# Three w2 tiles' differences moved from GpSimd to VectorE, and the sums of an output block as five operations instead of seven

## The chip, the cores and the metric

The program runs on one core of a Trainium2 chip. The time is the device time of one execution in microseconds (us). Engines are named as the profile names them: PE is TensorE, DVE is VectorE, ACT is ScalarE, POOL is GpSimd, SP is SyncE, which only issues DMAs here.

## The reference

Three layers follow each other: a windowed attention, a dense layer with a rational activation, and a layer of eight experts, in which the change lies:

```
def _moe2_ref(x, w_gate, w1, w2):          # 2304 tokens, 512 wide, 8 experts, 1024 hidden
    ...                                    # P: softmax of x @ w_gate, balanced 8 times
    for e in range(E):
        h = np.maximum(x @ w1[e], 0.0)
        ye = h @ w2[e]
        out += P[:, e:e + 1] * ye
    return out
```

## The kernel before

All products of the expert layer run on PE in half precision, each number split in a high and a low half (three matmuls stand for one), and each block product is done by a scheme of seven products on sums and differences of blocks, where the plain way takes eight.

**Blocks.** An expert is taken for three groups of 768 tokens; v counts the 24 pairs of expert and group. The 1024 hidden columns of an expert are cut into four slices, so that m = 4v + i counts 96 steps. A *unit* is one of seven products of layer 1 of a step: six matmuls of 384 columns (`moe_l1`, line L924). 28 units later (`LG`) layer 2 follows, three products to a unit: for each v three blocks of 128 token rows (p), for each the four slices i, for each seven products x of three matmuls of 256 columns (`moe_l2`, L1015 to L1017). L1015 takes the high halves of both operands, L1016 the low half of w2. So 84 units of both layers make one expert, and when layer 2 goes from one expert to the next (its *turn*), the four new w2 tiles must be there.

**Weights.** A tile of w1 or w2 is loaded into one of two buffers `raw0`, `raw1` (`raw_load`; L844 to L846 for w2). `raw_diff` (L873) makes its four differences in one buffer `wd`; `raw_split` makes the high halves on ACT (L884) and the low halves on DVE (L887), the three raw blocks first (768 columns), then the four differences (1024 columns). k counts an expert's tiles: 0 to 3 of w1, 4 to 7 of w2. The differences of expert 0 are DVE's, those of experts 1 to 7 POOL's: 224 operations. `pin` puts each of these behind the last h of its group that stands before it in the program: on DVE behind L991, on POOL behind POOL's L946, on ACT behind L990. Five buffers hold split w2 tiles, so tiles 5 to 7 of an expert can be filled only as the last block of the expert before is used up, and `use` and `prep_at` place their work there, three units apart. `raw_absmax` (L850) reads each tile once more, half an expert ahead.

**Layer 1's results** go from PE's banks through ACT (L973, L980) and DVE (L975, L978, L983), ReLU on ACT (L976, L984), sums by `combine` (L946: three on DVE, one on POOL), then high halves on ACT (L990) and low halves on DVE (L991). A bank takes its next product only when the earlier one has been read.

**Layer 2's results.** When the seven sums p1 to p7 of a block stand in four banks, `y_evac` adds them up: one copy on ACT (L1034), then on DVE seven additions of 256 columns (L1036), each of a bank's half and a block in SBUF. `y_out` scales the result on ACT (L1045) and adds it to the output by a DMA of POOL's queue (L1050). There are 72 such blocks. The four banks are handed to the next block as they come free.

The order of the instructions on each engine is made by a scheduler that plays the program through with costs of its own; each engine then works in that order.

Of the kernel before, what the change touches and what calls it, by code (L numbers as in the profile page):

```python
# [16 lines left out]
ALU = mybir.AluOpType  # L17
# [11 lines left out]
def kernel(  # L29
# [14 lines left out]
    nc = tc.nc  # L44
# [5 lines left out]
    P = 128  # L50
# [53 lines left out]
    def room(tag, shape, dt):  # L104
        where, era, a, size = HOME[tag]
        n = math.prod(shape[1:]) * (2 if dt == F16 else 4)
        assert n <= size, (tag, shape)
        old = rooms.get(where)
        if old is None or old[0] < era:
            old = rooms[where] = era, sb.tile([P, ROOMS[where] // 4], F32R if era == 1 else F32, tag=where, name=f"room{where}")  # L110
        assert old[0] == era, (tag, old[0])
        t = old[1][0:shape[0], a // 4:(a + n) // 4]
        if dt != (F32R if era == 1 else F32):
            t = t.bitcast(dt)
        d = "abcd"[:len(shape) - 1]
        if len(d) > 1:
            t = t.rearrange(f"p ({' '.join(d)}) -> p {' '.join(d)}", **dict(zip(d[1:], shape[2:])))
        return t
# [698 lines left out]
    NP = NF2 // 2  # L817
    FH = FE // 2
    EH = DM // 2
# [8 lines left out]
    def pin(eng, i):  # L828
        if eng in behind:
            tc.add_manual_dep(i.ins, behind[eng], mybir.DependencyInfo(mybir.DependencyClass.Sync, mybir.DependencyReason.DATA), reason="after this group's h")  # L830
# [36 lines left out]
    def raw_diff(e, k, n):  # L867
        w = k // NP
        o, x, y = DIFFS[w][n]
        d = room("wd", [P, 4, EH], F32)  # L870
        a, b = ({"b": raw[e, k], "d": d}[z[0]][:, int(z[1]), :] for z in (x, y))
        eng = nc.gpsimd if e else nc.vector
        pin("p" if e else "v", eng.tensor_tensor(out=d[:, o, :], in0=a, in1=b, op=ALU.add if w == 0 and n == 0 else ALU.subtract))  # L873

    def raw_split(e, k):
        w, i = divmod(k, NP)
# [116 lines left out]
    yb = {}  # L993
# [1 line left out]
    later_u = []  # L995
    unit_now = [0]
    gate_ready = [False]
    PRODS = ((0, 0, 1, 0), (0, 1, 5, 4), (1, 0, 4, 3), (1, 1, 6, 5), (2, 0, 3, 1), (2, 1, 7, 2), (3, 0, 2, 6))
    NQ = NM * 3 * 7

    def moe_l2(q):
        s, x = divmod(q, 7)
        v, r = divmod(s, 3 * NP)
        p, i = divmod(r, NP)
        e, G = GV[v]
        h = mac[v * NP + i]["h"]
        hh, hl = h[:, 0], h[:, 1]
        if i == 0 and x == 0:
            for b in range(4):
                yb[b] = bank("yps", True)  # L1010
        w = w2s[e, i]
        b, half, a, m = PRODS[x]
        o = yb[b][:, half * EH:(half + 1) * EH]
        c = slice(p * P, (p + 1) * P)
        nc.tensor.matmul(o, hh[:, a - 1, c], w[:, m, 0, :], start=i == 0 and half == 0, stop=False)  # L1015
        nc.tensor.matmul(o, hh[:, a - 1, c], w[:, m, 1, :], start=False, stop=False)  # L1016
        nc.tensor.matmul(o, hl[:, a - 1, c], w[:, m, 0, :], start=False, stop=i == NP - 1 and (half == 1 or b == 3))  # L1017
        if i == NP - 1 and x == 6:
            y_evac(v, p)
# [7 lines left out]

    def y_evac(v, p):
        yd = room(f"yd{(3 * v + p) % 2}", [P, 2, DM], F32)
        d = yd[:, 1, :], yd[:, 0, :]  # L1030
        vv = room("yv", [P, EH], F32)
        p1, p6, p5, p7, p2, p3, p4 = (yb[b][:, h * EH:(h + 1) * EH] for b, h, _, _ in PRODS)
        u, x, w, z = d[0][:, 0:EH], d[0][:, EH:], d[1][:, 0:EH], d[1][:, EH:]
        nc.scalar.activation(u, p1, AF.Copy)  # L1034
        for o, s0, s1 in ((vv, p6, u), (x, p5, vv), (w, p7, vv), (z, p7, x), (u, p2, u), (x, p3, x), (w, p4, w)):
            nc.vector.tensor_tensor(out=o, in0=s0, in1=s1, op=ALU.add)  # L1036
        if gate_ready[0]:
            y_out(v, p, yd)
        else:
            pend.append((v, p, yd))  # L1040

    def y_out(v, p, yd):
        e, G = GV[v]
        for n in range(2):
            nc.scalar.activation(yd[:, n, :], yd[:, n, :], AF.Copy, scale=gate_col(e, 2 * TPB * G + TPB * n + p))  # L1045
        dst = bass.AP(out.tensor, (2 * TPB * G + p) * P * DM, [[DM, P], [TPB * P * DM, 2], [1, DM]])
        if e == 0:
            nc.sync.dma_start(out=dst, in_=yd)
        else:
            later_u.append((unit_now[0] + 2, lambda: pin("p", nc.gpsimd.dma_start(out=dst, in_=yd, accum_op=ALU.add))))  # L1050
# [66 lines left out]
    for b, s0, s1 in ATT:  # L1117
        pcs = att_pieces(b)
        n = 4 * (s1 - s0 + 1) - 4
# [50 lines left out]
    def prep_at(s, e, k, step):  # L1170
        for n in range(4):
            at(int(s + n * step), raw_diff, e, k, n)
        for n in range(4):
            at(int(s + (1, 2, 4, 5)[n] * step), raw_part, e, k)
        use.append((int(s + 5 * step), e, k, s))
# [71 lines left out]
    n = len(pcs)  # L1247
# [92 lines left out]
```

## Time and profile before

| | |
|---|---|
| time, median of 3 runs | 2047.74 us (2046.5 to 2050.35) |
| the profiled execution's own time | 2048.93 us |
| its span, first to last instruction | 2047.1 us |
| busy: PE, DVE, ACT, POOL | 1904.1, 1635.2, 1230.9, 551.0 us |
| mean granted clock of PE | 0.967 of full speed |

The expert layer's products begin some 750 us into the span and last to its end. In the profile's slices by time PE is busy 90% or more from 800 us on and its granted clock is full. The end of a matmul is modelled there, past the start of the next, so that a busy PE can still start late; the starts in the timeline are what counts.

### The profile page before, as it was taken

To read this page: it belongs to the slowest core of one execution; us is meant where nothing else is said; L and a number is where in the kernel's file an instruction comes from. 1 tells how busy PE (TensorE), PEld (TensorE's weight loads), DVE (VectorE), ACT (ScalarE), POOL (GpSimd) and SP (SyncE) were. 2 spreads that over 40 slices of the span, in tenths; PEclk is the share of its full clock that TensorE was granted. 3 is DMA by queue.
4 is the path that set the end of the run, shared out by engine and by line. 5 is a ranking of instruction groups with operands and counts; after the bars stand their busy time and mean duration, and the time that the engine had idled before them with its cause. 6 is when DMAs were issued, how large, how long until landed. Compare 5 with 4: busy or idle time off the path is not lost. (4 is left out here: it accounts for less than half of the span.)

```text
span 2047.1 us, 36511 instructions
## 1 busy us (share of the span) xinstructions
PE 1904.1 (93%) x13914; PEld 1433.2 (70%) x13914; DVE 1635.2 (80%) x2844; ACT 1230.9 (60%) x2328; POOL 551.0 (27%) x574
## 2 busy tenths in 40 slices
PE   7588899998989789999999999999999999999997
PEld 6466667776766557777777777777777777777776
DVE  5898899899998878787777877877877787787754
ACT  5677777776776545555555654655565565465542
POOL 1232233222222003122332431422333143142211
PEclk7788999999999899999999999999999999999999
DMA  6542220124310333245346344435534634533323
GB/s 173 163 139 77 60 75 13 33 66 140 104 42 11 119 126 96 68 128 149 63 108 172 77 116 130 93 83 123 139 63 116 166 75 116 139 84 84 77 57 48
DMA packets 209792, 200.07 MB, mean 98 GB/s; under 512 B 78288, under 2 KB 160208, under 8 KB 209616
## 3 DMA queue, kind: packets, MB, share of 16 engines
q1 hardware_dynamic: 192480, 164.70, 26.4%
q0 software_dynamic: 17136, 33.03, 10.8%
q8 instruction: 109, 1.79, 0.4%
q14 instruction: 67, 0.55, 0.1%
HBM read 151.67 MB, written 46.01 MB: 97 GB/s over the span
## 5 line engine op out<-in xcount | busy, mean ns | idle before, releaser
L924 PEld LDWEIGHTS <-roomA 128*128 128x128 f16 x3276 | 322.1, 99 | 199.4 <-issue 36.5
L924 PE MATMUL l1a<-roomA 128*128 128x384 f16 x1872 | 357.3, 328 | 11.2 <-ACT roomA L973 5.3
L924 PE MATMUL l1b<-roomA 128*128 128x384 f16 x1404 | 277.0, 330 | 12.1 <-DVE roomA L975 6.7
L873 POOL TENSOR_TENSOR roomA<-roomA 128x256 f32<-128x256 f32 x224 | 198.3, 912 | 104.5 <-DVE roomA L887 62.2
L683 POOL TENSOR_TENSOR roomIG<-roomA,roomIG 128x384 fp32r<-128x384 f32 x96 | 112.9, 1176 | 295.2 <-ACT roomIG L682 238.7
L1015 PE MATMUL yps<-roomA 128*128 128x256 f16 x630 | 170.5, 272 | 5.8 <-ACT roomA L884 3.8
L1016 PE MATMUL yps<-roomA 128*128 128x256 f16 x630 | 171.1, 273 | 3.4 <-DVE roomA L887 3.3
L1015 PE MATMUL yps<-roomA,roomV 128*128 128x256 f16 x630 | 171.2, 273 | 1.4 <-DVE roomA L1036 0.8
L1016 PE MATMUL yps<-roomA,roomV 128*128 128x256 f16 x630 | 171.5, 273 | 0.0
L1017 PE MATMUL yps<-roomA 128*128 128x256 f16 x630 | 170.4, 273 | 1.0 <-DVE roomA L991 1.0
L1017 PE MATMUL yps<-roomA,roomV 128*128 128x256 f16 x630 | 170.9, 273 | 0.0
L645 PE MATMUL h1ps<-roomA 128*128 128x384 f16 x384 | 130.8, 341 | 16.0 <-DVE roomA L665 8.1
L698 PE MATMUL o1ps<-roomIG,roomV 128*128 128x384 f32 x384 | 137.9, 359 | 5.2 <-POOL roomIG L683 4.9
L946 POOL TENSOR_TENSOR roomIG<-roomA 128x384 f32<-128x384 f32 x48 | 57.1, 1190 | 313.8 <-ACT roomA L980 235.1
L699 PE MATMUL o1ps<-roomIG,roomV 128*128 128x384 f32 x384 | 131.4, 342 | 0.0
L646 PE MATMUL h1ps<-roomA 128*128 128x384 f16 x384 | 130.5, 340 | 0.0
L647 PE MATMUL h1ps<-roomA 128*128 128x384 f16 x384 | 130.2, 339 | 0.0
L887 DVE SCALAR_TENSOR_TENSOR roomA<-roomA,sm 128x768 f16<-128x768 f32 (+1 forms) x92 | 118.0, 1300 | 10.8 <-ACT roomA L884 8.0
L697 PE MATMUL o1ps<-roomIG,roomV 128*128 128x384 f32 x384 | 107.7, 382 | 16.3 <-ACT roomIG L682 14.6
L1016 PEld LDWEIGHTS <-roomA 128*128 128x128 f16 x1008 | 98.6, 98 | 30.5 <-issue 7.4
L884 ACT ACTIVATE roomA<-roomA,sm 128x768 f16<-128x768 f32 (+1 forms) x92 | 93.5, 1036 | 43.6 <-POOL roomA L873 18.9
L1015 PEld LDWEIGHTS <-roomA 128*128 128x128 f16 x1008 | 98.6, 98 | 29.5 <-issue 6.3
(215 smaller groups left out, 5035.9 us busy)
## 6 DMA issues: line engine op xcount, KB each, us to landing
roomA<-xd SPq DMA_DIRECT2D x119, 384.0 KB
roomA<-in_moe_w_dram SPq DMA_DIRECT2D x256, 128.0 KB
roomA<-in_moe_w_dram SPq DMA_DIRECT2D x128, 256.0 KB
out_dram<-roomV POOLq DMA_DIRECT2D x32, 512.0 KB, 6.0
out_dram<-roomA POOLq DMA_DIRECT2D x31, 512.0 KB, 5.8
roomV<-in_moe_w_in_dram SPq DMA_DIRECT2D x16, 512.0 KB
roomA<-in_moe_w_out_dram SPq DMA_DIRECT2D x16, 512.0 KB
xd<-roomA SPq DMA_DIRECT2D x14, 384.0 KB
```

What stands on the lines that cost most here:

```text
L645: mm = nc.tensor.matmul(hp, whi, xb[:, 0, kk, :], start=kk == 0, stop=False)
L646: nc.tensor.matmul(hp, whi, xb[:, 1, kk, :], start=False, stop=False)
L647: nc.tensor.matmul(hp, wlo, xb[:, 0, kk, :], start=False, stop=kk == KD - 1)
L683: nc.gpsimd.tensor_tensor(out=gl, in0=g, in1=gh.bitcast(F32), op=ALU.subtract)
L698: nc.tensor.matmul(ob[dd], hi, d["gl"], start=False, stop=False)
L699: nc.tensor.matmul(ob[dd], lo, d["gh"], start=False, stop=last)
L873: pin("p" if e else "v", eng.tensor_tensor(out=d[:, o, :], in0=a, in1=b, op=ALU.add if w == 0 and n == 0 else ALU.subtract))
L887: pin("v", nc.vector.scalar_tensor_tensor(out=l, in0=x, scalar=sc, in1=h, op0=ALU.mult, op1=ALU.subtract))
L924: mm = nc.tensor.matmul(ps, w[:, wx_, wh, kk * P:(kk + 1) * P], x[:, xh, kk, :], start=start and kk == 0 and wh == 0 and xh == 0, stop=sto ...
L1015: nc.tensor.matmul(o, hh[:, a - 1, c], w[:, m, 0, :], start=i == 0 and half == 0, stop=False)
L1016: nc.tensor.matmul(o, hh[:, a - 1, c], w[:, m, 1, :], start=False, stop=False)
L1017: nc.tensor.matmul(o, hl[:, a - 1, c], w[:, m, 0, :], start=False, stop=i == NP - 1 and (half == 1 or b == 3))
```

## The change

`raw_diff` gives POOL, for experts 1 to 7, only the differences of the four w1 tiles and of the first w2 tile (k = 4). The differences of tiles 5, 6 and 7, twelve operations for each of seven experts, go to DVE, and `pin` there puts them behind DVE's L991. In `PRODS` p7 and p5 change places, so that p7 and p5 fill one bank in this order. `y_evac` does five additions: p6 to u; p7 and p5 to the same block at once (2 x 256 columns, with a step of three blocks in the output); p7 to x; p2 and p3 at once (512 columns); p4.

```diff
-        eng = nc.gpsimd if e else nc.vector
-        pin("p" if e else "v", eng.tensor_tensor(out=d[:, o, :], in0=a, in1=b, op=ALU.add if w == 0 and n == 0 else ALU.subtract))
+        pool = e and (w == 0 or k == NP)
+        eng = nc.gpsimd if pool else nc.vector
+        pin("p" if pool else "v", eng.tensor_tensor(out=d[:, o, :], in0=a, in1=b, op=ALU.add if w == 0 and n == 0 else ALU.subtract))
...
-    PRODS = ((0, 0, 1, 0), (0, 1, 5, 4), (1, 0, 4, 3), (1, 1, 6, 5), (2, 0, 3, 1), (2, 1, 7, 2), (3, 0, 2, 6))
+    PRODS = ((0, 0, 1, 0), (0, 1, 5, 4), (1, 0, 6, 5), (1, 1, 4, 3), (2, 0, 3, 1), (2, 1, 7, 2), (3, 0, 2, 6))
...
-        d = yd[:, 1, :], yd[:, 0, :]
         vv = room("yv", [P, EH], F32)
-        p1, p6, p5, p7, p2, p3, p4 = (yb[b][:, h * EH:(h + 1) * EH] for b, h, _, _ in PRODS)
-        u, x, w, z = d[0][:, 0:EH], d[0][:, EH:], d[1][:, 0:EH], d[1][:, EH:]
+        p1, p6, _, _, _, _, p4 = (yb[b][:, h * EH:(h + 1) * EH] for b, h, _, _ in PRODS)
+        p75, p23 = (yb[b].rearrange("p (n c) -> p n c", n=2) for b in (1, 2))
+        q4 = yd.rearrange("p n (h c) -> p (n h) c", h=2)
+        w, z, u, x = (q4[:, i, :] for i in range(4))
         nc.scalar.activation(u, p1, AF.Copy)
-        for o, s0, s1 in ((vv, p6, u), (x, p5, vv), (w, p7, vv), (z, p7, x), (u, p2, u), (x, p3, x), (w, p4, w)):
-            nc.vector.tensor_tensor(out=o, in0=s0, in1=s1, op=ALU.add)
+        nc.vector.tensor_tensor(out=vv, in0=p6, in1=u, op=ALU.add)
+        nc.vector.tensor_tensor(out=q4[:, 0:4:3, :], in0=p75, in1=vv.unsqueeze(1).to_broadcast([P, 2, EH]), op=ALU.add)
+        nc.vector.tensor_tensor(out=z, in0=p75[:, 0, :], in1=x, op=ALU.add)
+        nc.vector.tensor_tensor(out=q4[:, 2:4, :], in0=p23, in1=q4[:, 2:4, :], op=ALU.add)
+        nc.vector.tensor_tensor(out=w, in0=p4, in1=w, op=ALU.add)
```

The scheduler orders the program anew, and line numbers after L870 grow by one, after L1030 by more (L873 becomes L874, L887 L888, L946 L947, L991 L992; the five additions are L1037 to L1041).

**First place**: DVE at the turn to expert 3, from the first half of tile 7's low halves (L887, 3x256) to the second (4x256). Before:

```order
L887 SCALAR_TENSOR_TENSOR roomA<-roomA,sm 128x3x256
L1036 TENSOR_TENSOR roomA<-yps,roomA 128x256 x2
L983 TENSOR_TENSOR roomA<-l1b,roomA 128x384
L887 SCALAR_TENSOR_TENSOR roomV_6434<-roomA,sm,roomV_6434 128x4x256
L946 TENSOR_TENSOR roomIG<-roomA 128x384
L946 TENSOR_TENSOR roomIG<-roomIG,roomA 128x384
L991 TENSOR_TENSOR roomA<-roomA 128x1152
L946 TENSOR_TENSOR roomIG<-roomA,roomIG 128x384
L978 TENSOR_TENSOR roomV_6583<-l1b,roomV_6583 128x384
L991 TENSOR_TENSOR roomA<-roomIG,roomA 128x1536
L887 SCALAR_TENSOR_TENSOR roomA<-roomA,sm 128x4x256
```

In the changed program, ending with the same L887 (now L888, 4x256); the L874 are the differences of tiles 6 and 7:

```order
L947 TENSOR_TENSOR roomIG<-roomA 128x384
L874 TENSOR_TENSOR roomA<-roomA 128x256
L947 TENSOR_TENSOR roomIG<-roomIG,roomA 128x384
L947 TENSOR_TENSOR roomIG<-roomA,roomIG 128x384
L992 TENSOR_TENSOR roomA<-roomA 128x1152
L888 SCALAR_TENSOR_TENSOR roomV_6434<-roomA,sm,roomV_6434 128x4x256
L992 TENSOR_TENSOR roomA<-roomIG,roomA 128x1536
L979 TENSOR_TENSOR roomV_6583<-l1b,roomV_6583 128x384
L874 TENSOR_TENSOR roomA<-roomA 128x256 x2
L976 TENSOR_TENSOR roomA<-l1b,roomA 128x384
L874 TENSOR_TENSOR roomA<-roomA 128x256 x2
L888 SCALAR_TENSOR_TENSOR roomA<-roomA,sm 128x4x256
```

The differences now stand in DVE's queue between the sums of layer 1, and tile 7's four come right ahead of the ScalarE and VectorE operations that split them. On PE, from the first matmul of the unit m = 40, product 0, up to the first matmul on the high halves of tile 7's differences, there stood 58 matmuls of 384 columns and 66 of 256; now there are 84 and 72, the last 24 of the 84 directly ahead of it. The first matmul on their low halves is now the fourth after that one. The counts are the same at all seven turns.

**Second place**: DVE at the sums of block v = 10, p = 1, while expert 4's w1 tile 2 is split. Before:

```order
L1036 TENSOR_TENSOR roomA<-yps,roomV_6583 128x256
L991 TENSOR_TENSOR roomA<-roomIG,roomA 128x1536
L1036 TENSOR_TENSOR roomV_6583<-yps,roomA 128x256 x2
L1036 TENSOR_TENSOR roomV_6583<-yps,roomV_6583 128x256
L887 SCALAR_TENSOR_TENSOR roomA<-roomA,sm 128x3x256
L1036 TENSOR_TENSOR roomV_6583<-yps,roomV_6583 128x256 x2
L978 TENSOR_TENSOR roomV_6583<-l1b,roomV_6583 128x384
L975 TENSOR_TENSOR roomA<-l1b,roomA 128x384
L887 SCALAR_TENSOR_TENSOR roomA<-roomA,sm 128x4x256
L1036 TENSOR_TENSOR roomV_6583<-yps,roomV_6583 128x256
L983 TENSOR_TENSOR roomV_6583<-l1b,roomV_6583 128x384
```

In the changed program:

```order
L1037 TENSOR_TENSOR roomA<-yps,roomV_6583 128x256
L992 TENSOR_TENSOR roomA<-roomIG,roomA 128x1536
L1038 TENSOR_TENSOR roomV_6583<-yps,roomA 128x2x256
L888 SCALAR_TENSOR_TENSOR roomA<-roomA,sm 128x3x256
L976 TENSOR_TENSOR roomA<-l1b,roomA 128x384
L1039 TENSOR_TENSOR roomV_6583<-yps,roomV_6583 128x256
L1041 TENSOR_TENSOR roomV_6583<-yps,roomV_6583 128x256
L979 TENSOR_TENSOR roomV_6583<-l1b,roomV_6583 128x384
L888 SCALAR_TENSOR_TENSOR roomA<-roomA,sm 128x4x256
L1040 TENSOR_TENSOR roomV_6583<-yps,roomV_6583 128x512
L984 TENSOR_TENSOR roomV_6583<-l1b,roomV_6583 128x384
```

The sum on p2 and p3 is one operation and the last of the block (before, p3's was the last, and p2's stood ahead). On PE the first matmul that waits for this bank stands three matmuls of 384 columns earlier than before.

**Third place**: DVE ahead of the last ACT operation of step m = 42, where L850 waits for a load of expert 4's tiles. Before:

```order
L850 TENSOR_REDUCE sm<-roomA 128x1 x2
L200 TENSOR_REDUCE sm<-sm 128x1
L983 TENSOR_TENSOR roomV_6583<-l1b,roomV_6583 128x384
L850 TENSOR_REDUCE sm<-roomA 128x1
L946 TENSOR_TENSOR roomIG<-roomV_6583 128x384
L991 TENSOR_TENSOR roomV_6693<-roomV_6583,roomV_6693 128x1152
L946 TENSOR_TENSOR roomIG<-roomIG,roomV_6583 128x384
L946 TENSOR_TENSOR roomIG<-roomV_6583,roomIG 128x384
```

In the changed program:

```order
L850 TENSOR_REDUCE sm<-roomA 128x1 x2
L200 TENSOR_REDUCE sm<-sm 128x1
L984 TENSOR_TENSOR roomV_6583<-l1b,roomV_6583 128x384
L947 TENSOR_TENSOR roomIG<-roomV_6583 128x384
L947 TENSOR_TENSOR roomIG<-roomIG,roomV_6583 128x384
L850 TENSOR_REDUCE sm<-roomA 128x1
L992 TENSOR_TENSOR roomV_6693<-roomV_6583,roomV_6693 128x1152
L947 TENSOR_TENSOR roomIG<-roomV_6583,roomIG 128x384
```

Two of the three sums of step 42 (L946, now L947) move ahead of the last L850; before, all three stood behind it.

## Rows read from the trace of the kernel before

**Rows 1.** the page's busy time of each engine, share of the span, instructions.
```profile
PE 1904.1 (93%) x13914; PEld 1433.2 (70%) x13914; DVE 1635.2 (80%) x2844; ACT 1230.9 (60%) x2328; POOL 551.0 (27%) x574
```

**Rows 2.** PE's waits from 780 us on: us in total, times, longest.
```profile
PE l1a L924 <- ACT roomA L973: 5.9, 6, 2.3
...
PE yps L1015 <- ACT roomA L884: 3.8, 4, 1.5
...
PE yps L1016 <- DVE roomA L887: 3.3, 4, 0.8
...
PE yps L1015 <- ACT roomV L884: 1.8, 2, 1.0
...
PE yps L1016 <- DVE roomV L887: 1.6, 2, 0.8
```

**Rows 3.** timeline of PE at expert 3's turn: start, length, [idle before].
```profile
1212.13 1.14 PE L924 MATMUL l1a<-roomA 128*128 128x384 f16 x6
...
1227.79 0.27 PE L1015 MATMUL yps<-roomA 128*128 128x256 f16 x1
...
1228.12 0.81 PE L924 MATMUL l1b<-roomA 128*128 128x384 f16 x4
...
1229.76 0.38 PE L1015 MATMUL yps<-roomA 128*128 128x256 f16 x2 [0.83 <-ACT roomA L884]
...
1232.54 0.27 PE L1016 MATMUL yps<-roomA 128*128 128x256 f16 x1 [0.82 <-DVE roomA L887]
```

**Rows 4.** timeline of VectorE, GpSimd and ScalarE at expert 3's turn.
```profile
1209.13 1.76 DVE L991 TENSOR_TENSOR roomV<-roomIG,roomV 128x1536 f16<-128x1536 f32 x1 [1.14 <-ACT roomV L990]
...
1219.15 1.28 DVE L887 SCALAR_TENSOR_TENSOR roomV<-roomA,sm,roomV 128x1024 f16<-128x1024 f32 x1
...
1221.11 1.04 DVE L946 TENSOR_TENSOR roomIG<-roomA 128x384 f32<-128x384 f32 x1 [0.67 <-ACT roomA L984]
...
1221.67 3.55 POOL L873 TENSOR_TENSOR roomA<-roomA 128x256 f32<-128x256 f32 x4
...
1222.18 2.45 DVE L946 TENSOR_TENSOR roomIG<-roomIG,roomA 128x384 f32<-128x384 f32 x1
...
1224.55 1.88 DVE L991 TENSOR_TENSOR roomA<-roomA 128x1152 f16<-128x1152 f32 x1
...
1226.35 0.55 DVE L946 TENSOR_TENSOR roomIG<-roomA,roomIG 128x384 f32<-128x384 f32 x1
...
1228.50 1.76 DVE L991 TENSOR_TENSOR roomA<-roomIG,roomA 128x1536 f16<-128x1536 f32 x1 [1.14 <-ACT roomA L990]
...
1228.56 1.15 ACT L884 ACTIVATE roomA<-roomA,sm 128x1024 f16<-128x1024 f32 x1
...
1230.37 2.12 DVE L887 SCALAR_TENSOR_TENSOR roomA<-roomA,sm 128x1024 f16<-128x1024 f32 x1
```

**Rows 5.** groups by form, whole span: busy us, mean ns.
```profile
L873 DVE TENSOR_TENSOR roomA<-roomA 128x256 f32<-128x256 f32 x32 | 13.5, 442 | 0.0
...
L1036 DVE TENSOR_TENSOR roomA<-yps,roomA 128x256 f32<-128x256 f32 x252 | 94.3, 415 | 11.5 <-PE yps L1017 5.9 <-ACT roomA L1034 4.7
...
L983 DVE TENSOR_TENSOR roomV<-l1b,roomV 128x384 f32<-128x384 f32 x48 | 26.5, 553 | 45.3 <-PE l1b L924 45.2
```

**Rows 6.** timeline of VectorE: four L1036 in a row.
```profile
1215.31 1.41 DVE L1036 TENSOR_TENSOR roomA<-yps,roomA 128x256 f32<-128x256 f32 x4
```

**Rows 7.** timeline of VectorE and PE ahead of m = 44.
```profile
1264.87 1.22 DVE L850 TENSOR_REDUCE sm<-roomA 128x1 f32<-128x1024 f32 x1 [4.02 <-DMA roomA<-in_moe_w_dram]
...
1266.47 1.35 DVE L991 TENSOR_TENSOR roomV<-roomV,roomV 128x1152 f16<-128x1152 f32 x1
...
1270.89 1.14 PE L924 MATMUL l1a<-roomA 128*128 128x384 f16 x6 [0.84 <-ACT roomA L973]
```

**Rows 8.** timeline of VectorE and PE at a sum's last operation.
```profile
1318.66 0.42 DVE L1036 TENSOR_TENSOR roomV<-yps,roomV 128x256 f32<-128x256 f32 x1
...
1319.13 0.27 PE L1015 MATMUL yps<-roomA 128*128 128x256 f16 x1 [0.31 <-DVE roomV L1036]
```


## The prediction

> **What bounds the kernel now.** I read the page first: PE is busy 93% of the span, DVE 80%, POOL 27% [rows 1]. From 780 us on, where the change lies, PE is nearly full. A unit there is six matmuls of 384 columns and nine of 256. Their pitch is in the timeline: a 256-column matmul starts 0.11 us after the one ahead (three from 1227.79 to 1228.12; I use 0.109), and six of 384 columns last 0.33 us longer than four, 0.16 to 0.17 each, of which I use 0.163 [rows 3]. The matmuls themselves cannot get shorter, so what can be won is only the time that PE loses between them. A faster DVE or POOL is worth nothing where PE does not wait for it.
>
> So I next read PE's waits, which name the loss [rows 2]. Twelve waits are for split weights: on ACT's L884 (3.8 + 1.8 us, six waits) and on DVE's L887 (3.3 + 1.6, six waits), 10.5 us in all. Six more are for L973 on ACT (5.9 us). The ends of matmuls are modelled too late: at expert 3's turn four matmuls start at 1228.12, the next was due at 1228.12 + 4 x 0.163 = 1228.77 and came at 1229.76, 0.99 late, where the row has 0.83 of idle time [rows 3]. So I add 0.16 to each wait: 12.4 us lost for weights, 6.9 for L973. The first pair is one L884 and one L887 in each of the six turns to experts 2 to 7, about 2.07 us a turn.
>
> **Why PE waits at a turn.** The timeline of the other engines at expert 3's turn shows the last tile's chain [rows 4]. POOL makes its four differences from 1221.67 to 1225.22. In that time DVE's L946 on two operands in SBUF takes 1.04 and 2.45 us, where one without POOL beside it takes 0.55 us, and L991 on 1152 columns takes 1.88 where it takes 1.35 elsewhere [rows 4, 7]. So the last sum of that step ends only at 1226.90, DVE idles 1.14 us for ACT, L884 on the differences, which stands behind that step on ACT, starts at 1228.56, and L887 runs from 1230.37 to 1232.49. PE starts on the high halves at 1229.76 and on the low ones at 1232.54 [rows 3].
>
> The Trainium skill, page SBUF — State Buffer, section Who interferes with whom, says that a DVE instruction with two SBUF inputs and a GpSimd instruction that reads SBUF lock each other out for a whole instruction. The trace agrees in the 2.45 us. The rule also cuts against the change, since the moved differences have two SBUF inputs and POOL keeps its own L946; that is a rival below.
>
> **The changed turn, step by step.** I start from the last L887's start before, 1230.37, and change what the new order changes on DVE after L991 at 1209.13 [rows 4].
> - Added: eleven of the twelve differences (the first stands far ahead). One on DVE takes 0.442 us as a mean of expert 0's 32 [rows 5]. Four L1036 of 0.415 us fit into 1.41 us [rows 5, 6], so starts are 0.33 apart, and each overlaps the next by 0.08. I take 0.36 a difference: +4.0 us. Bounds: 0.33 (as L1036), and 0.89, POOL's own pace here (3.55 / 4 [rows 4]).
> - Added: one L975 that now stands ahead, of a kind with L983 (0.553 [rows 5], pitch 0.47): +0.5.
> - The sums of a block: seven starts of 0.33 = 2.3 us become three of 0.33 and two of 512 columns. From 0.415 at 256 and 0.553 at 384 columns [rows 5] I extrapolate 0.69, pitch 0.61: 2.2 us, -0.1. Bounds for one: 0.47 (as 384 columns) and 0.66 (two of 256).
> - Removed: the stretch beside POOL's differences, (2.45 - 0.55) + (1.04 - 0.55) + (1.88 - 1.35) = -2.9.
> - Waits: the 1.14 us ahead of L991 goes, since its sum is no longer late: -1.1. L887 must now wait for ACT's L884 (1.15 us and some 0.3 of queue), as the differences stand right ahead of it on its own engine: +1.4.
>
> The last L887 starts at 1230.4 + 4.0 + 0.5 - 0.1 - 2.9 + 0.3 = 1232.2 and, with 1.28 less 0.08 [rows 4], is done at 1233.4. The L884 ends when the L887 starts, 1232.2.
>
> When does PE ask? In the order before, 58 x 0.163 + 66 x 0.109 = 16.65 us after 1212.13 [rows 3], at 1228.78, and the trace showed it waiting from there. In the changed order it is 84 x 0.163 + 72 x 0.109 = 21.54 us: 1233.67 for the high halves and three matmuls later, 1234.0, for the low ones. So the chain ends some 2 us later than before in position and PE asks 4.9 us later: the high halves have 1.4 us to spare, the low ones 0.6. The work that fills the gap is layer 1's, which is needed anyway. I leave 0.2 us of lateness a turn: of 12.4 us, 1.2 stay, **-11.2 us**. Between the bounds: with 0.33 a difference nothing stays (-12.4); with 0.89 the chain is 5.8 later, 5.2 too late, 31 us over six turns (+19).
>
> The Trainium skill, VectorE: DVE Perf Modes, section The DRAIN you can't avoid, says that the next DVE operation starts only when the pipeline has run empty. Full durations would put eleven differences at 4.9 us, leave the low halves 0.3 us late, and make this term -10.6. The four L1036 in 1.41 us speak against it [rows 6]; its section Two Vector instructions with no wait between them allows the earlier start that they show.
>
> **The other terms.** (a) The L973 waits: the timeline ahead of m = 44 has L850 waiting 4.02 us for a load, then three L946 and one L991 behind it, then ACT, and PE late by 0.84 + 0.16 [rows 7]. With two L946 ahead of L850, the chain behind the load is about 1.05 us shorter (0.47 and, with its small gap, 0.58), which covers five of six waits and part of the longest: at most -5.5. The load itself may land at another time, so I take half, -2.8 (bounds 0 and -5.5). (b) The sum over p2 and p3 is now last in its block, and PE asks for its bank three matmuls (0.49 us) earlier. Its predecessor there started at 1318.66 and PE lost 0.31 + 0.16 [rows 8]; now the operation is 0.27 longer (0.69 against 0.42). +0.76 each, in five blocks of this kind (experts 1 to 4 and 6): +3.8 at most; I take +3.0, as p4's bank now comes free ahead of it (bounds 0 and 3.8). (c) DVE's sums shrink by some 0.1 us a block, 72 blocks; elsewhere PE does not wait for them, so they count nothing. If that cover went, it would be 7 us of DVE time, spread thin. (d) POOL loses 84 operations, 27% busy as it is [rows 1]; what it ends is the chain above, and nothing else here.
>
> Sum: -11.2 - 2.8 + 3.0 = -11.0. Against the profiled execution's own 2048.93 us that is 2037.9; the median of the runs, 2047.74, is 1.2 lower, so **2037 us** (-0.5%). About 0.2% (4.1 us) is what a measurement of this kernel can tell from no change.
>
> **Rivals.**
> - *DVE becomes the late chain (slower).* The differences wait in DVE's queue behind L991, and the L887 that PE needs stands behind them; whatever delays one delays all. The point: when the chain is later by 0.6 + 2.07 = 2.7 us than reckoned, a difference costing 0.60 instead of 0.36, the gain is gone. At 0.75 it is 4.3 - 0.6 = 3.7 us a turn, 22 over six turns, +9.8, with (a) and (b) 2058. For it: in the new order VectorE does eleven operations more between the same two points. Against: the operation that stretched it most, POOL's four differences beside it, is gone there.
> - *The lock stays (GpSimd's L946 against the moved differences).* POOL's L946 at this turn falls on DVE's last L887, 2.12 us against 1.28 [rows 4]: 0.84 lost. This is the section on interference named above. Two such meetings a turn cost 1.7 - 0.6 = 1.1 us, 6.6 over six turns: -5.8 instead of -11.2, 2042. I count it with the forecast's low gain.
> - *The waits move (no change).* The scheduler's order asks at other places as late as things come: half of the turn's lateness stays (6.2), (a) gives nothing and (b) its full 3.8: -2.4, 2045.
> - *All of it goes.* -12.4 - 5.5 and no new wait at the banks: -17.9, 2030.
>
> **How the numbers follow.** The forecast with the lock's share, 2031 to 2043.6: 0.50. All of it goes, below 2031: 0.09. The waits move, 2043.6 to 2051.8: 0.22. DVE late, above 2051.8: 0.19. Faster 0.59, no change 0.22, slower 0.19. The range 2030 to 2053 leaves out 0.05 below and 0.14 above; the forecast's own is 2031 to 2044.
>
> **What would show it.** PE's waits on L884 and L887 near 2 us or less instead of 10.5; DVE's L946 back at 0.55 at the turns, with a difference on DVE near 0.42 us; POOL busy some 76 us less; L973's waits about half; the waits on the block sums up by some 3 us. I am wrong if PE still stands at the turns for L887, if the moved differences take 0.6 us or more, or if waits of the same size appear at L1 banks in the four units run ahead.

## The result

| | before | after |
|---|---|---|
| time, median | 2047.76 us (2046.5 to 2050.35) | 2025.52 us (2023.24 to 2032.67) |
| span of the profiled execution | 2047.1 us | 2023.9 us |
| ratio to before, 95% interval | | 0.9896 [0.9869, 0.9922] |

The change is faster by 1.0%, twice what was forecast, and the time lies below the range. The busy time of the page answers [rows 1]:

```profile
PE 1896.6 (94%) x13914; PEld 1428.6 (71%) x13914; DVE 1625.1 (80%) x2784; ACT 1235.8 (61%) x2328; POOL 486.8 (24%) x490
```

POOL lost 64 us (forecast some 76), and DVE, which took over the differences, is no busier. The groups by form over the whole span (busy us, mean ns) answer [rows 5]:

```profile
L874 POOL TENSOR_TENSOR roomA<-roomA 128x256 f32<-128x256 f32 x140 | 130.1, 948 | 37.3 <-DVE roomA L888 23.6 <-DVE roomV L888 9.2 <-issue 1.2
L874 DVE TENSOR_TENSOR roomA<-roomA 128x256 f32<-128x256 f32 x116 | 46.3, 420 | 0.5
...
L1040 DVE TENSOR_TENSOR roomV<-yps,roomV 128x512 f32<-128x512 f32 x36 | 24.6, 684 | 0.0
...
L1037 DVE TENSOR_TENSOR roomA<-yps,roomV 128x256 f32<-128x256 f32 x36 | 15.0, 418 | 9.0 <-ACT roomV L1036 8.9
```

A difference takes DVE 0.42 us and POOL 0.95; a sum of 512 columns takes 0.684, near the 0.69 reckoned. PE's waits from 780 us on answer [rows 2] (us in total, times, longest):

```profile
PE yps L1016 <- DVE roomV L1040: 2.2, 3, 0.7
PE yps L1016 <- DVE roomA L1040: 2.2, 3, 0.7
PE l1b L925 <- DVE roomV L976: 1.7, 6, 0.3
...
PE l1a L925 <- ACT roomV L974: 0.9, 4, 0.3
PE l1b L925 <- DVE roomA L979: 0.8, 3, 0.3
```

No wait for split weights is left, and none of the six long ones for L973 (now L974). In their place stand six waits for the sum on p2 and p3 (L1040) and some short ones of layer 1. VectorE's wait for the load of a raw tile, to which the prediction traced the long ones, before and after:

```profile
DVE sm L850 <- DMA roomA<-in_moe_w_dram: 25.0, 6, 5.4
```

```profile
DVE sm L850 <- DMA roomA<-in_moe_w_dram: 12.9, 6, 2.5
```

The timeline at expert 3's turn, PE, DVE and ACT together, answers [rows 3, 4]:

```profile
1205.87 1.14 PE L925 MATMUL l1a<-roomA 128*128 128x384 f16 x6
...
1222.07 0.88 DVE L874 TENSOR_TENSOR roomA<-roomA 128x256 f32<-128x256 f32 x2
...
1223.41 1.14 ACT L885 ACTIVATE roomA<-roomA,sm 128x1024 f16<-128x1024 f32 x1
...
1224.59 1.28 DVE L888 SCALAR_TENSOR_TENSOR roomA<-roomA,sm 128x1024 f16<-128x1024 f32 x1 [1.64 <-ACT roomA L885]
...
1227.38 0.49 PE L1016 MATMUL yps<-roomA 128*128 128x256 f16 x3
```

The first row is the first matmul of m = 40, from which the prediction counts. The last low halves start 18.72 us after it (before 18.24; forecast some 2 us more), PE asks for the high halves after 21.51 us (forecast 21.54), and it does not wait.

For the whole expert stage I use one measure below, **lateness**: every start of a matmul against the one ahead, less the pitch (0.163 us for 384 columns, 0.109 for 256), where more than 0.15 us is left, summed over the trace from 770 us on. It is 35.4 us before and 16.1 after. The profile of before holds another 5.4 us: the first unit of layer 1 starts at 638.5 us of the span there and at 633.1 after. That part is scatter: a second profile of each gave 637.3 and 636.6, and all the runs together spread from 632.1 to 640.5.

Of before's 35.4 us, 1.4 are no wait. PE's clock was not full through the whole stage: behind the longest wait for L973 (2.25 us), matmuls of 384 columns started 0.32 us apart for some 3 us, and the granted clock there (the third number from the end) was half, 1.2 of 2.4 GHz:

```profile
1613.40:1616.40 3.00, 3.00 (x11) 1.41 (x10) 3.00 (x5) 0.32 (x1) 0.99 (x1) 0.50 0.02 5
```

After has no such stretch between 780 us and the last block, nor has the second profile of before.

### The profile page after: what moved, and what is told of

Read it like the earlier page. It is cut to its first block, busy times and chain, and to the rows that moved or that the text cites. A ratio compares the mean times of both kernels' runs of the same rounds, so it can differ in the third digit from the quotient of the medians.

```text
span 2023.9 us, 36375 instructions
## 1 busy us (share of the span) xinstructions
PE 1896.6 (94%) x13914; PEld 1428.6 (71%) x13914; DVE 1625.1 (80%) x2784; ACT 1235.8 (61%) x2328; POOL 486.8 (24%) x490
## 5 line engine op out<-in xcount | busy, mean ns | idle before, releaser
L925 PEld LDWEIGHTS <-roomA 128*128 128x128 f16 x3276 | 321.9, 99 | 197.6 <-issue 32.2
L947 POOL TENSOR_TENSOR roomIG<-roomA 128x384 f32<-128x384 f32 x48 | 60.7, 1264 | 464.4 <-ACT roomA L981 314.1
L874 POOL TENSOR_TENSOR roomA<-roomA 128x256 f32<-128x256 f32 x140 | 130.1, 948 | 37.3 <-DVE roomA L888 23.6
L888 DVE SCALAR_TENSOR_TENSOR roomA<-roomA,sm 128x768 f16<-128x768 f32 (+1 forms) x92 | 113.7, 1249 | 21.1 <-ACT roomA L885 19.8
L947 POOL TENSOR_TENSOR roomIG<-roomV 128x384 f32<-128x384 f32 x48 | 50.0, 1041 | 323.5 <-ACT roomV L981 304.7
L1016 PEld LDWEIGHTS <-roomA 128*128 128x128 f16 x1008 | 98.6, 98 | 30.6 <-DVE roomA L1040 3.7
L1017 PEld LDWEIGHTS <-roomV 128*128 128x128 f16 x1008 | 99.0, 98 | 25.0 <-issue 1.5
```

Source lines behind the costliest of these rows:

```text
L874: pin("p" if pool else "v", eng.tensor_tensor(out=d[:, o, :], in0=a, in1=b, op=ALU.add if w == 0 and n == 0 else ALU.subtract))
L888: pin("v", nc.vector.scalar_tensor_tensor(out=l, in0=x, scalar=sc, in1=h, op0=ALU.mult, op1=ALU.subtract))
L925: mm = nc.tensor.matmul(ps, w[:, wx_, wh, kk * P:(kk + 1) * P], x[:, xh, kk, :], start=start and kk == 0 and wh == 0 and xh == 0, stop=sto ...
```

## The experiments

All were timed against the kernel before on the same chip. Lateness is that of the profiled execution.

| run | what it is | us | ratio, 95% interval | lateness |
|---|---|---|---|---|
| e1 | differences alone | 2016.84 | 0.9847 [0.9832, 0.9862] | 4.7 |
| e2 | sums alone | 2030.19 | 0.9908 [0.9892, 0.9924] | 19.6 |
| e3 | the change again | 2028.29 | 0.9902 [0.9886, 0.9919] | 18.6 |
| e4 | before again | 2049.82 | one run | 36.0 |
| e5 | e1, idle work on POOL | 2017.69 | 0.9852 [0.9839, 0.9865] | 5.1 |
| e6 | e1, p7 and p5 as one | 2016.37 | 0.9845 [0.9832, 0.9858] | 4.7 |
| e7 | e1, p2 and p3 as one | 2031.64 | 0.9918 [0.9906, 0.9929] | 18.2 |
| e8 | the change, p4 ahead | 2029.18 | 0.9908 [0.9895, 0.9921] | 19.1 |
| e9 | e1, idle work on POOL that reads the raw tile | 2020.72 | 0.9862 [0.9847, 0.9877] | 7.4 |
| e10 | e1, p2 waits for p3 | 2015.93 | 0.9843 [0.9828, 0.9857] | 4.7 |
| e11 | the change, one more dependency | 2027.93 | 0.9901 [0.9884, 0.9917] | 16.8 |
| e12 | e1, no difference on POOL | 2016.90 | 0.9843 [0.9828, 0.9858] | 4.9 |
| e13 | the change in e1's order | 2015.64 | 0.9849 [0.9837, 0.9862] | 4.4 |
| e14 | e1 in the change's order | 2028.82 | 0.9915 [0.9903, 0.9927] | 16.6 |
| e15 | **before** in e1's order | 2015.97 | 0.9849 [0.9837, 0.9862] | 4.6 |
| e16 | e2 in before's order | 2040.51 | 0.9969 [0.9960, 0.9979] | 30.2 |
| e17 | e1 in before's order | 2079.98 | 1.0156 [1.0142, 1.0170] | 61.3 |
| e18 | **before** in the change's order | 2030.36 | 0.9904 [0.9886, 0.9921] | 16.6 |

Time less lateness is 2010 to 2014 us in every row but e17 (2019): lateness is nearly all that the kernels differ by. Most of what e17 has more, some 4 us, are 36 matmuls of 256 columns at half the granted clock, each 0.11 late and so under the measure's 0.15.

### The halves apart (e1 to e4)

Three theories stood. A: the gain is the turn's, and so the differences'. B: it comes from the sums. C: some 5 us of the first comparison lie ahead of the expert stage and are scatter. e1 has the diff's lines in `raw_diff` alone, e2 those in `PRODS` and `y_evac` alone.

> Only the differences of w2 tiles 5 to 7 on VectorE; the sums stay seven operations. Theory A (the late chain at the turn to a new expert was the loss, and the moved differences undo it): PE's waits on the split weights, 10.5 us before, are gone, and the time falls by 11 to 16 us, 2032 to 2037; what the whole change won beyond that is the sums'. Rival B (the gain comes from the sums and from the order that the scheduler makes with them): at most 5 us of gain, with waits of some 2 us a turn left on L884 and L887. Rival C (some 5 us of the 22 lie ahead of the expert layer and are variation between executions): the first layer-1 product of the experts starts anywhere between 632 and 639 us, whatever the kernel.

> Only the sums as five operations, with p7 and p5 exchanged; all differences of experts 1 to 7 stay on GpSimd. Theory A: the waits on the split weights at the turns stay near 10 us and the time is within 5 us of before, 2043 to 2050. Rival B: 10 us or more faster, 2037 or less.

> The changed kernel once more, on the same chip as the two halves. Theory A and B: 2022 to 2030. Rival C: its first layer-1 product of the experts starts later than the 633 us of the first profile, nearer to the 638 us of before; under A alone it starts at 633 us again, as the same program.

> The kernel before once more, with a profile. Rival C: its first layer-1 product of the experts starts at another time than the 638.5 us of the first profile, by some us. If it is 638 us again, the 5 us ahead of the expert layer belong to the change. From there to the end it should take the same 1398 us as before, within 2 us.

The differences alone gave 32 us, the sums alone 18.7, and both together 20.6, so neither A nor B holds as put. C holds in kind: the stage began at 638.5 and 637.3 us before, 633.1 and 636.6 after. From its start to the end e4 took 1410.7 us and the first profile of before 1408.6 (the 1398 of the expectation is a slip). In e1, PE waits six times in the whole stage:

```profile
PE yps L1016 <- DVE roomA L1037: 1.2, 2, 0.8
PE yps L1018 <- DVE roomA L992: 1.0, 1, 1.0
PE yps L1016 <- DVE roomV L1037: 0.6, 1, 0.6
PE yps L1016 <- ACT roomA L991: 0.4, 1, 0.4
PE l1a L925 <- ACT roomV L974: 0.3, 1, 0.3
```

From one expert's first block to the next it is 164.9 us, and 84 units of 6 x 0.163 + 9 x 0.109 us make 164.6: PE's own work fills it.

### GpSimd's work put back (e5, e9, e12)

Is it that POOL's slow results are late (theory W), or that DVE's operations stretch beside POOL (theory L)? e5 and e9 keep e1's program and PE's order and give POOL a subtraction for each one taken from it, whose result nobody reads.

```diff
+        if e and not pool:
+            s = masks.rearrange("p a k -> p (a k)").bitcast(F32)[:, 0:EH]
+            pin("p", nc.gpsimd.tensor_tensor(out=s, in0=raw[e, k][:, 0, :], in1=raw[e, k][:, 3, :], op=ALU.subtract))
```

That is e9; e5 has a constant for both operands. e12 sets `pool = False`.

> The differences are on VectorE as in the differences-only kernel (2016.8 us), the sums stay seven operations, and GpSimd does, at each place from which a difference was taken, a subtraction of the same size on constants whose result nobody reads; TensorE's instructions stand in the same order as in the differences-only kernel. Theory L (what GpSimd's work costs is that VectorE's operations beside it take longer): the stretching comes back to near the 66.9 us of before and the time to 2035 or more. Theory W (what costs is only that the low halves wait for GpSimd's slow results at the turn): nobody waits for these results, so the time stays at 2016 to 2021, the four late starts per turn stay away, and VectorE's stretching comes back without a price.

> As the kernel with GpSimd's replaced subtractions (2017.7 us), but here each of them reads two blocks of the raw tile, as GpSimd's differences of before did, so that it starts when those started and holds the raw buffer as long; its result is still read by nobody. Everything of before's GpSimd work is then back except that the low halves wait for its results. Theory W (the low halves' wait for GpSimd's results is the whole price): 2016 to 2021. Theory L (VectorE's operations stretched beside GpSimd, or the raw buffer held longer and the next load later): 2030 or more, with VectorE's wait for the raw tile's transfer back near the 25.0 us of before.

> All differences of all experts on VectorE, seven sums. Theory F (after the change of the differences TensorE has only 4.7 us of late starts left in this stage, and an expert takes 164.9 us whatever else is moved): 2014 to 2020, no gain over the differences alone although GpSimd does some 115 us less. Rival V (VectorE, 50 us fuller, becomes late): 2025 or more.

POOL is as busy in e9 as in before (its groups from 850 to 2000 us):

```profile
L877 POOL TENSOR_TENSOR masks<-roomA 128x256 f32<-128x256 f32 x84 | 84.0, 1000 | 7.1 <-DMA roomA<-in_moe_w_dram 0.7 <-POOL roomIG L950 0.2
```

The time stays at 2017.7 and 2020.7 against 2016.8. e9's 2.7 us of lateness more are mostly seven waits of 0.3 us for a block's sums. Not all of before came back with it: DVE's stretching (its durations above the shortest tenth of their form, from 850 to 2000 us) is some 47 us in e5 and 51 in e9, against 67 before and 36 in e1, and its wait for the raw tile's load, near 25.0 us under L, is 6.4 in e9. So L falls for what came back: POOL's presence costs 1 to 4 us in this order. W seemed shown at this point; e15 took that back. In e12 DVE does 224 operations more than before and POOL works 189 us less, and nothing is gained over e1, as F had it.

### Which part of the sums (e6, e7, e8, e10, e11)

e6 and e7 add to e1 one of the two operations of two results; e8 exchanges the last two of the change's sums; e10 makes the single sum on p2 wait for p3's matmuls; e11 puts the weights' work on DVE behind the sum on p2 and p3:

```diff
-        nc.vector.tensor_tensor(out=q4[:, 2:4, :], in0=p23, in1=q4[:, 2:4, :], op=ALU.add)
+        behind["v"] = nc.vector.tensor_tensor(out=q4[:, 2:4, :], in0=p23, in1=q4[:, 2:4, :], op=ALU.add).ins.name
```

> Differences on VectorE, sums as six operations: p7 and p5 with the shared sum in one operation of 512 columns, p2 and p3 apart. Theory Q (the part of the sums that costs is the operation on p2 and p3, which comes late, frees its bank late and pushes the last sum back): 2015 to 2020, as the differences alone. Rival R (any fused pair costs, since a 512-column operation takes 0.684 us at a stretch against 0.33 us steps of two small ones): 2021 or more.

> Differences on VectorE, sums as six operations: p2 and p3 in one operation of 512 columns, p7 and p5 apart. Theory Q: 2023 to 2030, near the whole change (2025 to 2028), with the waits of the next block's seventh product at 0.8 to 0.9 us an expert. Rival R: half of the way, about 2021. If instead it is 2015 to 2020, the cost of the sums lies in the p7 and p5 operation or in both together.

> The whole change, with the last two of the five sums exchanged (p4's sum ahead of the one on p2 and p3), so that the fourth bank comes free 0.68 us earlier and the third 0.42 us later; TensorE's order is the same as in the whole change. Theory B2 (the whole change loses against the differences alone mainly by its seventh product's waits for the fourth bank, 5.7 us in all): these waits go, the fifth product's grow by less than 0.4 us an expert, and the time falls by 3 to 6 us against the whole change, to 2020 to 2024. Rival (the loss lies in the order of TensorE's work that the five operations bring, not in the bank): no more than 1.5 us less than the whole change.

> Differences on VectorE, seven sums, and the sum on p2 made to wait for the matmuls of p3 as well, as the one operation on both must. TensorE's instructions stand in the order of the differences-only kernel. Theory R1 (the operation on p2 and p3 costs because it can't start until both are there): 2025 or more. Theory O (it costs because the scheduler, with this operation, lays the engines' queues in another order): 2015 to 2020, with no more than 1 us of late starts at the next block's seventh product.

> The whole change with one more dependency: the weights' work on VectorE (absolute maximum, differences, low halves) that is issued after a block's sums in the program must stand behind the operation on p2 and p3. The number of times that a low half stands directly ahead of this operation falls from 6 to 1, and TensorE's order changes too. Theory O (the loss against the differences alone lies in the order of the queues): most of the 9 to 12 us come back, 2016 to 2021. Rival P (it lies in the operation itself: its 0.684 us or the bank that it holds): 2025 or more.

p7 and p5 as one cost nothing, as theory Q (only the operation on p2 and p3 costs) had it; p2 and p3 as one cost 15 us, a little over its range. But e7's waits are not at that operation alone (PE, from 780 us on):

```profile
PE l1a L925 <- ACT roomA L974: 5.6, 6, 1.3
PE l1b L925 <- DVE roomV L976: 1.9, 6, 0.3
PE yps L1016 <- DVE roomV L1041: 1.5, 3, 0.5
PE yps L1016 <- DVE roomA L1041: 1.5, 3, 0.5
```

The six waits of before at L974 are back, and DVE's waits for the raw tile's load with them:

```profile
DVE sm L850 <- DMA roomA<-in_moe_w_dram: 22.8, 6, 4.1
```

e8 turned out to be the change once more: the scheduler orders these two sums by itself, and every engine's queue is the same, row for row. In the change, too, p4's sum stands ahead of the one on p2 and p3. So the change has three medians, 2025.5, 2028.3 and 2029.2, and no theory was tried by e8. e10 kept e1's order and cost nothing, so it is not that p2 has to wait. e11 took the waits for a block's sums in the later experts away (5.6 us of lateness to 0.2) and got 6.5 us at layer 1's first step of experts 2 to 7; by its time alone the rival P (the operation costs by itself) was right, but it too had a new order. Each of these edits had changed two things: the instructions and every queue.

### The order held (e13 to e18)

At the end of the program, each of these adds to every instruction the dependency on the one that stands ahead of it, on its engine, in another kernel. `ORDER` holds the row numbers of all five engines.

```
for e, z in ORDER.items():
    ...
    for a, b in zip(got, got[1:]):
        tc.add_manual_dep(b, a.name, mybir.DependencyInfo(mybir.DependencyClass.NoSync, mybir.DependencyReason.DATA), reason="order")
```

> The whole change, all five sums, but every engine's queue held, row for row, in the order of the differences-only kernel (each operation of two results stands where the later of its two single ones stood, the one on p7 and p5 ahead of the sum that uses it). Theory O (what the sums lose is the other order that the scheduler gives every queue): 2014 to 2020, as the differences alone (2016.8). Rival P (the operation on two results costs by itself): 2024 or more.

> The differences on VectorE and the seven sums of before, every queue held in the order of the changed kernel (each pair of single sums stands where its operation of two results stood). Theory O: the changed kernel's time, 2024 to 2031, with its late starts at the last sums and at the tenth group, though no sum of two results is left. Rival P: 2014 to 2020.

> The kernel before, with its differences on GpSimd and its seven sums, every queue held in the order of the differences-only kernel; the 84 differences go back into GpSimd's queue after the instruction behind which they stood in before. Theory W (the price is the low halves' wait for GpSimd's slow results, whatever the order): 2040 or more, with TensorE's waits at the turns back at 9 us or more. Rival O2 (before's order of the queues made most of the price): 2030 or less.

> The five sums alone, differences on GpSimd, every queue held in the order of before. Theory O3 (the 18.7 us that the sums alone gave came from the new order of the queues; the five operations as such free VectorE of 0.27 us a block and no more): 2044 to 2051. Rival S (the shorter sums themselves took the waits away): 2035 or less.

> The differences on VectorE and nothing else, every queue held in the order of before; each moved difference stands in VectorE's queue as early as it may, behind the low half of the tile before it and behind the units' work that it must follow. The prediction's own terms for this edit (11.2 at the turns, 2.8 at the L973 waits): 2031 to 2036, with the four late starts at each turn gone and the other waits of before still there. Theory O (the order of the queues is the price, the engine of the differences is not): 2042 or more.

> The kernel before, unchanged differences on GpSimd and seven sums, every queue held in the order of the changed kernel. Theory O: the changed kernel's time without any of its edits, 2023 to 2032. Rival E (in this order the edits are needed, since the low halves wait for GpSimd again): 2036 or more.

| order of the queues | before's instructions | differences on DVE | the whole change |
|---|---|---|---|
| of before | 2047 | 2080.0 (e17) | |
| of the change | 2030.4 (e18) | 2028.8 (e14) | 2025.5 to 2029.2 |
| of e1 | 2016.0 (e15) | 2016.8 (e1) | 2015.6 (e13) |

Theory O (the order of the queues is the price, not the instructions) holds in e13, e14 and e18, and so does O2 in e15. In the last two rows, within an order, all three kernels take the same time, to 5 us in the order of the change and to 1 us in e1's. Between these orders it is 10 to 14, and both beat before's, with before's own instructions. The kernel before, with nothing changed but the order, is as fast as any kernel that was run. e15's differences are POOL's, and at expert 3's turn they are slow (PE, POOL, ACT and DVE together):

```profile
1203.95 1.14 PE L924 MATMUL l1a<-roomA 128*128 128x384 f16 x6
...
1217.32 4.41 POOL L873 TENSOR_TENSOR roomA<-roomA 128x256 f32<-128x256 f32 x4 [1.89 <-DVE roomV L887]
...
1217.65 2.00 DVE L991 TENSOR_TENSOR roomA<-roomIG,roomA 128x1536 f16<-128x1536 f32 x1 [0.42 <-ACT roomA L990]
...
1221.77 1.15 ACT L884 ACTIVATE roomA<-roomA,sm 128x1024 f16<-128x1024 f32 x1 [2.07 <-POOL roomA L873]
...
1222.95 1.28 DVE L887 SCALAR_TENSOR_TENSOR roomA<-roomA,sm 128x1024 f16<-128x1024 f32 x1 [2.82 <-ACT roomA L884]
...
1224.48 0.49 PE L1015 MATMUL yps<-roomA 128*128 128x256 f16 x3
```

The four take 4.41 us, the low halves start 19.00 us after the first matmul of m = 40, later than before (18.24) and than after (18.72). PE comes for the high halves at 20.53 us and does not wait, for 150 matmuls stand ahead instead of 124; after has 156. With before's 124 (16.65 us) PE would have come some 2 us before they were there (an estimate from these rows). W falls: the low halves' wait for POOL is a price only where PE asks early.

In e18, with POOL's differences and seven sums in the order of the change, no wait for split weights is left either, and rival E falls (PE, from 780 us on):

```profile
PE yps L1015 <- DVE roomV L1036: 3.0, 4, 1.3
PE yps L1015 <- DVE roomA L1036: 2.8, 5, 0.7
PE l1b L924 <- DVE roomV L975: 1.9, 6, 0.3
```

e14 has seven plain sums and waits where the change waited, at the sums and at layer 1:

```profile
PE yps L1016 <- DVE roomV L1037: 3.0, 4, 1.3
PE yps L1016 <- DVE roomA L1037: 2.8, 5, 0.7
PE l1b L925 <- DVE roomV L976: 1.9, 6, 0.3
```

So the 9 to 12 us that the change loses against e1 are its order's and not the operation's on p2 and p3; e11's rival P falls with that. In before's order the edits do matter. The sums give 6 us there (e16, between the two expectations: the waits for weights stay, 13.8 us of lateness). The differences cost 33 us. That lies within theory O's "2042 or more", but its reason, that the engine of the differences is not the price, does not hold there, and the prediction's terms (2031 to 2036) fail. `pin` holds a moved difference behind DVE's L992, and in before's order that is late. Expert 3's turn in e17 (DVE and ACT):

```profile
1241.56 1.76 DVE L992 TENSOR_TENSOR roomA<-roomIG,roomA 128x1536 f16<-128x1536 f32 x1 [1.14 <-ACT roomA L991]
...
1243.36 0.42 DVE L874 TENSOR_TENSOR roomA<-roomA 128x256 f32<-128x256 f32 x1
...
1243.88 1.15 ACT L885 ACTIVATE roomA<-roomA,sm 128x1024 f16<-128x1024 f32 x1 [2.35 <-DVE roomA L874]
```

The fourth difference alone stands there, and PE waits for the high halves 2.5 us at the worst. The raw buffer is held longer too, so SP's queue stands at L844 for DVE's difference, up to 15.3 us at a time; in before it stood there for POOL's, up to 6.4. Before, then e17:

```profile
SPq L844 <- POOL roomA L873: 131.4, 28, 6.4
```

```profile
SPq L844 <- DVE roomA L874: 104.4, 7, 15.3
```

Behind it in that queue are layer 1's inputs, which PE then lacks (PE's waits):

```profile
PE l1b L925 <- DMA roomA<-xd: 15.6, 7, 2.6
PE yps L1016 <- ACT roomA L885: 9.1, 5, 2.5
```

The waits for layer 1's inputs make 16.7 us of lateness. Those for weights make 13.8 (before 12.4). And behind seven waits of 2.0 to 2.5 us the granted clock fell to half for 3.4 us each time, where before has one such stretch: 12 us of the 33 against 1.7. One of the seven:

```profile
1054.30:1057.60 3.30, 3.30 (x12) 1.52 (x10) 2.95 (x8) 0.00 (x0) 0.00 (x0) 0.50 0.89 303
```

Where the moved differences stand in before's order was for this run to choose; they stand as early as they may, and other places were not tried.

Two things stay open. No run held a kernel in its own order; that the holding itself costs and gives nothing rests on e13 and e14, which take the times of e1 and of the change. And all five queues were held together, so that no run shows which of them matters.

## Why the prediction was wrong

The direction was right and the size half. Its own steps, as lateness of before and after:

- **The turn, -11.2:** 12.4 us became none, -12.4, and the step's numbers held: PE's asking time to 0.03 us, a difference at 0.42 us in steps of 0.33 to 0.46, no wait for weights. But the cause was put in the wrong place. Of the three that the step names (faster differences, the stretch beside POOL gone, layer 1's matmuls run ahead), e15 shows that the first two are not needed: with POOL's differences and their stretch the low halves come in time too. The matmuls run ahead are what is left of the three; that they do it is read from e15's rows, since e15 held the other queues as well.
- **(a) The L973 waits, -2.8:** 6.9 us became none, then 1.4 and 2.1 in the repeats of the same queues: -4.8 to -6.9. The bound was -5.5, and the step took half of it, because the load might land later. It did not: DVE's waits at L850 fell from 25.0 us to 12.9. This term was mis-sized. The half clock behind the longest of these waits went with it, -1.4, and was no term of the sum.
- **A term that was not there:** before has seven more waits for L973, of 0.3 us each, one as layer 1 goes to each new expert. Their line stands among those from which the prediction took its own [rows 2], and it took nothing for it:

```profile
PE l1a L924 <- ACT roomV L973: 2.3, 7, 0.4
```

  They are 3.5 us of lateness, and after has none: -3.5.
- **(b) The bank of p2 and p3, +3.0:** at that place 2.4 us became 5.4, +3.0. That is luck in part: each wait grew by 0.43 us and not by 0.76, and a sixth block came to the five. The other waits at a block's sums in these experts (4.3 us) went, and 4.5 us came new at the eleventh of an expert's twelve layer 1 steps and 1.3 at the ninth; none of these was a term.
- **(c), DVE's shorter sums, no value:** it does not hold in before's own order. The five sums alone gave 6 us there (e16), and the waits for L973 lost 3.8 us of lateness, though the prediction says that PE does not wait for these sums elsewhere. In the orders of e1 and of the change they give nothing (e13 against e1, the change against e14).
- **(d), POOL's fewer operations, no value:** e5, e9, e12 and e15 bear that out, to 4 us.

-12.4 - 6.9 - 1.4 - 3.5 + 3.0 - 4.3 + 4.5 + 1.3, and 0.4 in the first expert and the last block, make -19.3, against 19.4 measured (35.44 - 16.08) and -11.0 forecast. The rest of the miss, some 3 us, is scatter: the first comparison was the fastest of the change's three. The range failed because its fast end was that of one rival, in which only the priced waits go.

Under all of this lies the step of method that failed: the prediction took before's list of waits and priced the edit against it, and took up the new order only at three places. But the scheduler had written all queues anew, and the time went with the queues: before's instructions in the order of the change take 2030.4 us. Why it writes another order when some differences move or one sum is fused is not in a trace; that stays open. The rival that DVE becomes the late chain, in which a difference stands in its queue behind L991, names the place at which e17 loses, but not its path: the differences still took 0.42 us, the waits for weights at the turns grew by 1.4 us only, and the loss came by the raw buffer, SP's queue, layer 1's inputs and the clock. The new order removed it.

## What to carry to other kernels

Where a scheduler orders the queues, an edit is two changes: the instructions and the order. Run the edit in the old order and the old kernel in the new order before anything is said of a cause; here the second alone had the change's gain (a ratio of 0.9904 in e18, 0.9896 to 0.9908 in the change's three comparisons) and, in e1's order, e1's (0.9849 in e15, 0.9847 in e1). A stall of PE has two ends: in e15 it closed with no faster producer, where work that PE has to do anyway stood ahead of the late operand. When the loss of a stage is 5 us, stop moving work between the other engines: e5, e6, e10, e12, e13 and e15 all end at 2016 to 2018 us.

## What the runs showed of the hardware

POOL and DVE hold each other in both directions. In e15 the four differences beside DVE's L991 took 4.41 us (the second of them 2.23, the other three 0.72 each), and that L991 took 2.00 us where after has 1.75 for the same form with no POOL operation beside it. The Trainium skill, SBUF — State Buffer, section Who interferes with whom, gives such a lock for two-input DVE operations beside GpSimd's, and the traces agree with it. But the stretch had no price in e1's order: e15 has some 42 us of it (measured as for e5 and e9), e1 has 36, and both take 2016 to 2017 us.

A long wait of PE can cost more than itself. In e17 seven waits of 2.0 to 2.5 us had stretches of 3.4 us at a granted clock of 0.50 behind them, in before one of 2.25 us had; others as long (2.63 us at 1574.8 us in e17) had none, and e1 and e15 show no such stretch from 780 us to the last block.
